# Rectified units made from two ScalarE reads of the PSUM bank and one VectorE instruction, in the first three blocks of a fused attention and two-layer kernel

## The chip, the cores and the metric

The kernel runs on one core of one Trainium2 chip. The metric is device time in microseconds (us), from one launch. A run is one execution; the number for a kernel is the median of its runs. One more execution, taken by the hardware profiler, gives the trace: a record of each instruction with its engine, start and duration. The engines are TensorE (PE, with its weight loads PEld), VectorE (DVE), ScalarE (ACT), GpSimd (POOL) and SyncE (SP), and each works through its own instructions strictly in order. "SPq" and "ACTq" rows are the issues of DMAs on those engines' queues.

## What is computed

Causal attention with a bias made from running sums, then two feed-forward layers on the 2304 tokens (4 sequences of 576, 512 columns). The change is in the second layer, where `h` is rectified with a slope `alpha` of its own for each of the 2048 hidden columns:

```python
# first layer: 1536 hidden columns
a = x @ w_a
b = x @ w_b
x = a * b @ w_out
# second layer: 2048 hidden columns
h = x @ w_in
g = np.maximum(h, 0.0) + alpha * np.minimum(h, 0.0)
return (g @ w_out).astype(np.float32)
```

## The kernel before

The tokens go through the two layers in four blocks: three of 512 tokens (function `ffn`) and one of 768 (`ffn_seven`). The attention of block b+1 is cut into steps that are dealt out between the matrix products of block b; only the first block's attention stands alone, in the first 49 us. Every number that enters a large product is split into a high part (rounded to the matmul's type) and the rest, so `x`, `g` and the weights are pairs (`xh`/`xl`, `gh`/`gl`, `wh`/`wl`) and one product is three matmuls: L1237 to L1239 in the helper `mm3`, or L1888 to L1890 where the second layer leaves its result with tokens on partitions.

In one block the first layer takes 12 turns and the second 16. A turn `f` of the second layer is `into(f % 2)`: 12 matmuls of 512 columns that write `h` for 128 hidden columns into one of two PSUM banks, bank2 for even f and bank3 for odd f (`ab[0]`, `ab[1]`; in the instruction lists below their names end in `_101` and `_102`); then, from the third turn on, the 12 matmuls of the product with `w_out` for turn f-2. PE may write a bank again only when `used[j]`, the chain that reads it, is done. With two banks and two turns before the first `w_out` product, the third turn needs bank2 back while the second is computed; later turns have 12 more matmuls in between.

The chain that reads the bank is `rectify` (L1833 to L1846): ScalarE writes `m = relu(-h)` from the bank (`act`, L286), the helper `scale` (L321) multiplies `m` by `-alpha` on VectorE or GpSimd, and VectorE's scalar_tensor_tensor (L302) reads the bank a second time and makes `g = max(h, 0) + m`. After it `split_g` makes `gh` on ScalarE (L294) and `gl` on VectorE or GpSimd (L311). `m`, `g`, the first layer's `a_sb` and the results `o` that go out share four buffers (`ft`, tag "t", slots `of_t`).

The order of instructions on every engine is set when the program is built, by a planner (class `Order`): every operation has a planned cost on each engine that may do it, is given to the engine that would end it first, and takes its place in the lists by planned start. Operations marked `dve2` hold, with GpSimd's, a common resource "port" in the plan; those marked `dve` don't. A change of one planned cost can so reorder all that is planned after it, and also pick another engine for operations that the change doesn't name. Weights arrive in the first block as 64-bit numbers (`raw<-in_w_dram`), are decoded by ACT (`top`, L1018) and DVE (`raw` or `w`, L302), split into `wh`/`wl`, and stored back to DRAM (`w_d<-raw`, `w_d<-w`, on ACT's queue) for the later blocks. All loads and the stores of results are on SP's queue, in order.

The fourth block has a `rectified_parts` of its own (L1443), which already makes both halves on ScalarE, with `less_alpha = -alpha`, computed at L1316 when that block opens.

Of the kernel before, what the change touches and what calls it, by code (L numbers as in the profile page):

```python
# [15 lines left out]
AF = mybir.ActivationFunctionType  # L16
ALU = mybir.AluOpType
# [204 lines left out]
def attention_two_moe_kernel(  # L222
# [10 lines left out]
    nc = tc.nc  # L233
# [41 lines left out]
    run = Order()  # L275
# [5 lines left out]
    def size(ap):  # L281
        return prod(ap.shape[1:])

    def act(o, i, func=AF.Copy, **k):
        yield {"act": run.act + 0.833 * size(o) + 93 * len(set(k) - {"scale"})}, SEEN
        nc.scalar.activation(o, i, func, **k)  # L286
# [13 lines left out]
    def dve(n, rate, f, *args, port=False, **k):  # L300
        yield {"dve2" if port else "dve": run.dve + rate * n}, SEEN
        f(*args, **k)  # L302

    def either(pool, dve2):
        return {"dve2": dve2} if run.no_pool else Either(pool=pool, dve2=dve2)
# [12 lines left out]
    def scale(o, i, s0, s1):  # L318
        n = size(o)
        eng = yield either(115 + 1.09 * n, dve2=run.dve + 0.52 * n), SEEN  # L320
        (nc.gpsimd if eng == "pool" else nc.vector).tensor_scalar(  # L321
            o, i, s0, s1, op0=ALU.mult, op1=ALU.mult
        )
# [27 lines left out]
    less_alpha = small.tile([P, NF2], F32, name="less_alpha", bufs=1)  # L351
    alpha_sb = small.tile([P, NF2], F32, name="alpha_sb", bufs=1)
# [32 lines left out]
    for i in range(0, P, BH):  # L385
# [4 lines left out]
        op1=ALU.mult,  # L390
# [278 lines left out]
    def both(b, hp, rs):  # L669
        for j in range(2):  # L670
            biases(b, 2 * hp + j, rs)
# [213 lines left out]
    def first_attention():  # L885
        nonlocal ahead
        s_sb = work.tile([BH, S], F32, name="s_sb", tag="z4")
        for i in range(WARM):
            nc.tensor.matmul(acc[0][:, 0:P], ident, ident, start=True, stop=True)
        nc.scalar.activation(alpha_sb[:, 0:1], ident[:, 0:1], AF.Exp)  # L890
        nc.sync.dma_start(s_sb, s)
        for i in range(2):
            load_kq(0, i, 0)
        run.now = 2000.0
        run.pump()
        ahead = EARLY_TILES
        prefetch()
        run.now = 3000.0
        run.pump()
        for i in range(2, HP):  # L900
            load_kq(0, i, 0)
        load_v(0)
        run.pump()
        running_sums(s_sb)
        run.now = 5000.0
        lead, steps = plan[0]

        def scores(i):
            both(0, i, (0, 1))
            both(0, i, (2,))  # L910
            both(0, i, (3,))
            s01(0, i)
            s23(0, i, 2)
            s23(0, i, 3)

        def turns(i):
            for c in range(3):
                for j in range(2):
                    turn(0, 2 * i + j, c)

        def of_steps(n):
            for f, args in steps[:n]:
                f(*args)
            del steps[:n]

        scores(0)
        nc.sync.dma_start(alpha_sb, alpha)
        nc.sync.dma_start(cum_d, cum[0:BH, 0:S])
        scores(1)
        ahead = AHEAD  # L930
        prefetch()
        f, args = lead.pop(0)
        f(*args)
        scores(2)
        turns(0)
        scores(3)
        for x, j in ((xh, "h"), (xl, "l")):
            x.append(xp.tile([P, KD, 512], F32R, name=f"x{j}1", tag=f"x{j}1"))
        for f, args in lead:
            f(*args)  # L940
        turns(1)
        av(0, 0)
        turns(2)
        av(0, 1)
        turns(3)
        av(0, 2)
        of_steps(STEPS)
        av(0, 3)
        of_steps(STEPS)

    def attention(a):

# [354 lines left out]
    def open_seven():  # L1307

        inner.close()
        big = ctx.enter_context(tc.tile_pool(name="big", bufs=1))  # L1310

        def big_tile(shape, dtype, tag, bufs=1):
            return big.tile(shape, dtype, name=tag, tag=tag, bufs=bufs)

        pools["big"] = big_tile
        nc.vector.tensor_scalar(less_alpha, alpha_sb, -1.0, None, op0=ALU.mult)  # L1316
        t_hl[:] = [
            [big_tile([P, 2, H2], F32R, f"t{j}{i}") for j in "hl"] for i in range(4)
        ]
        for slots, n in ((of_m, 4), (of_a22, 2), (of_mt, 2), (of_st, 2), (of_d, 5)):  # L1320
            for _ in range(n):
                run.give(slots)
# [465 lines left out]
    def ffn(blk):  # L1788
        T = sizes[blk]
# [43 lines left out]
        def rectify(f, hp):  # L1833
            yield of_t
            m = ft.tile([P, T], F32, name="m", tag="t")
            yield from act(m, hp, AF.Relu, scale=-1.0)
            yield from scale(m, m, alpha_sb[:, f:f + 1], -1.0)
            yield of_t
            g = ft.tile([P, T], F32, name="g", tag="t")
            yield from dve(  # L1840
                T, 1.04, nc.vector.scalar_tensor_tensor, g, hp, 0.0, m, op0=ALU.max, op1=ALU.add
            )
            run.give(of_t, run.t)
            split_g(f, g)
# [61 lines left out]
    for blk in range(NB):  # L1906
# [5 lines left out]
        T = sizes[blk]  # L1912
# [78 lines left out]
```

## Time and profile before

| | us |
|---|---|
| median of 3 runs | 982.25 |
| lowest and highest run | 981.21, 983.04 |
| the profiled execution's own time | 982.93 |
| its span, first to last instruction | 981.1 |

| engine | busy us | share of the span |
|---|---|---|
| PE | 965.5 | 98% |
| DVE | 748.9 | 76% |
| ACT | 551.6 | 56% |
| POOL | 224.8 | 23% |

Busy shares are means over the whole program. The blocks follow each other at about 49, 265, 500 and 706 us, and the second layers of the first three begin at about 162, 385 and 611 us. A matmul's record is longer than the time to the next one's start, because they are pipelined; what PE lost is read from the starts.

### The profile page before, as it was taken

What the parts mean: (1) busy time and instruction counts of PE and PEld (TensorE: products, weight loads), DVE (VectorE), ACT (ScalarE), POOL (GpSimd) and SP (SyncE); (2) the same over time, 40 slices, a digit from 0 to 9 for tenths busy, and PEclk for the clock granted to TensorE, in tenths of its full rate; (3) what the DMA queues carried; (4) which work ended last, traced back from release to release, by engine and by line L of the source; (5) the groups of instructions that cost most, each with busy time, mean ns of one, the idle gap of its engine ahead of it and who ended that gap; (6) DMA issues with size and microseconds to landing.
All of it is one profiled execution on the core that took longest, in us unless ns stands there. A gap on an engine that the chain in (4) does not pass through costs nothing.

```text
span 981.1 us, 15781 instructions
## 1 busy us (share of the span) xinstructions
PE 965.5 (98%) x5267; PEld 811.4 (83%) x5267; DVE 748.9 (76%) x1714; ACT 551.6 (56%) x1155; POOL 224.8 (23%) x286
## 2 busy tenths in 40 slices
PE   7999999999999999999999999999999999999997
PEld 6677877788878887888888888888899999999896
DVE  8897869877779788777577667975597888787782
ACT  7866766666656556644455455654452333576453
POOL 3141112311245254722044243640000000000000
PEclk9999999999999999999999999999999999999999
DMA  7489997989899898485696867445313223021202
GB/s 264 135 294 328 371 353 243 320 278 330 268 324 299 261 319 252 160 277 168 180 280 202 268 211 221 163 156 164 116 34 96 65 65 104 27 65 65 65 1 64
DMA packets 128065, 192.69 MB, mean 196 GB/s; under 512 B 34288, under 2 KB 65520, under 8 KB 127984
## 3 DMA queue, kind: packets, MB, share of 16 engines
q1 hardware_dynamic: 118192, 173.86, 55.5%
q10 hardware_dynamic: 9792, 17.83, 4.9%
q8 instruction: 41, 0.67, 0.3%
q14 instruction: 40, 0.33, 0.1%
HBM read 148.06 MB, written 43.59 MB: 195 GB/s over the span
## 4 chain that ended last, share of the span: by engine, by line
PE 89%; DVE 4%; DMA 4%; ACT 2%; issue 1%; ACTq 0%; SPq 0%; POOL 0%; POOLq 0%; DVEq 0%
PE bank L1237 20%; PE bank L1238 20%; PE bank L1239 20%; PE bank L1888 4%; PE bank L1889 4%; PE bank L1890 4%; PE bank L842 3%; PE bank L1741 2%; PE bank L1740 2%; PE bank L1742 2%; PE bank L579 2%; DMA cb<-cum_d 1%; DMA raw<-in_w_dram 1%; PE bank L777 1%; DVE z L302 1%; PE bank L869 1%
## 5 line engine op out<-in xcount | busy, mean ns | idle before, releaser
L1237 PE MATMUL bank<-xh,wh 128*128 128x512 f32 (+1 forms) x620 | 238.7, 385 | 4.9 <-ACT a_sb L294 1.7
L1238 PE MATMUL bank<-xl,wh 128*128 128x512 f32 (+1 forms) x620 | 234.3, 378 | 0.0
L1239 PE MATMUL bank<-xh,wl 128*128 128x512 f32 (+1 forms) x620 | 234.3, 378 | 0.0
L294 ACT ACTIVATE wh<-raw 128x512 fp32r<-128x512 f32 (+1 forms) x199 | 116.6, 594 | 145.6 <-PE bank L1238 59.1
L1237 PEld LDWEIGHTS bank<-xh,wh 128*128 128x128 f32 x620 | 116.4, 188 | 29.8 <-issue 3.0
L311 DVE TENSOR_TENSOR wl<-raw,wh 128x512 fp32r<-128x512 f32 (+1 forms) x148 | 97.3, 670 | 51.5 <-ACT wh L294 50.8
L1239 PEld LDWEIGHTS bank<-xh,wl 128*128 128x128 f32 x620 | 116.4, 188 | 19.5
L1238 PEld LDWEIGHTS bank<-xl,wh 128*128 128x128 f32 x620 | 116.5, 188 | 18.4
L286 ACT ACTIVATE z<-z,mn 128x128 f32<-128x128 f32 (+4 forms) x144 | 82.7, 576 | 20.1 <-DVE mn L302 19.4
L311 POOL TENSOR_TENSOR wl<-raw,wh 128x512 fp32r<-128x512 f32 x56 | 75.5, 1349 | 69.7 <-ACT wh L294 64.4
L1237 PE MATMUL bank<-gh,wh 128*128 128x512 f32 (+1 forms) x240 | 90.3, 376 | 0.0
L1238 PE MATMUL bank<-gl,wh 128*128 128x512 f32 (+1 forms) x240 | 88.8, 370 | 0.1
L1239 PE MATMUL bank<-gh,wl 128*128 128x512 f32 (+1 forms) x240 | 88.5, 369 | 0.0
L1888 PE MATMUL bank<-wh,gh 128*128 128x512 f32 x192 | 77.0, 401 | 0.0
L1889 PE MATMUL bank<-wl,gh 128*128 128x512 f32 x192 | 74.9, 390 | 0.0
L1890 PE MATMUL bank<-wh,gl 128*128 128x512 f32 x192 | 74.9, 390 | 0.0
L1018 ACT ACTIVATE top<-raw 128x512 f16<-128x512 bf16 x82 | 63.2, 785 | 20.1 <-DMA raw<-in_w_dram 18.5
L311 DVE TENSOR_TENSOR gl<-g,gh 128x512 fp32r<-128x512 f32 x70 | 55.6, 795 | 20.2 <-ACT gh L294 19.7
L294 ACT ACTIVATE gh<-g 128x512 fp32r<-128x512 f32 x83 | 51.9, 625 | 30.2 <-DVE g L302 28.3
L311 POOL TENSOR_TENSOR wl<-w,wh 128x512 fp32r<-128x512 f32 x26 | 35.1, 1354 | 113.9 <-ACT wh L294 84.6
L302 DVE STREAM_TRANSPOSE zt<-z 128x384 f32<-128x384 f32 (+2 forms) x88 | 55.5, 647 | 3.1 <-DMA zd<-zt 2.0
L652 POOL TENSOR_SCALAR_AFFINE_SELECT z<-z 128x128 f32<-128x128 f32 (+2 forms) x80 | 34.4, 438 | 97.2 <-DVE z L642 47.0
(156 smaller groups left out, 1930.0 us busy)
## 6 DMA issues: line engine op xcount, KB each, us to landing
raw<-w_d SPq DMA_DIRECT2D x95, 512.0 KB, 4.6
raw<-in_w_dram SPq DMA_DIRECT2D x82, 512.0 KB, 6.4
w_d<-w ACTq DMA_DIRECT2D x54, 256.0 KB, 6.2
kq<-in_kq_a_dram SPq DMA_DIRECT2D x24, 512.0 KB, 5.9
zd<-zt SPq DMA_DIRECT2D x48, 192.0 KB, 4.1
pt<-zd SPq DMA_DIRECT2D x48, 192.0 KB, 4.7
zd<-zt SPq DMA_DIRECT2D x24, 256.0 KB, 2.7
pt<-zd SPq DMA_DIRECT2D x24, 256.0 KB, 4.9
```

Source lines behind the costliest of these rows:

```text
L286: nc.scalar.activation(o, i, func, **k)
L294: nc.scalar.activation(o, i, AF.Copy, scale=by)
L302: f(*args, **k)
L311: (nc.gpsimd if eng == "pool" else nc.vector).tensor_tensor(o, i0, i1, op=ALU.subtract)
L652: nc.gpsimd.affine_select(d, d, pattern=pattern, base=0, channel_multiplier=1, compare_op=ALU.is_ge, fill=MASKED,)
L1018: nc.scalar.activation(top.bitcast(F16).rearrange("p (n t) -> p n t", t=2)[:, :, 1], r.bitcast(BF16)[:, 4:4 + 4 * WN].rearrange("p (n t) - ...
L1237: nc.tensor.matmul(o, wh, ih, start=first, stop=False)
L1238: nc.tensor.matmul(o, wh, il, start=False, stop=False)
L1239: nc.tensor.matmul(o, wl, ih, start=False, stop=last)
L1888: nc.tensor.matmul(acc[t], gh[:, c], wh, start=first, stop=False)
L1889: nc.tensor.matmul(acc[t], gh[:, c], wl, start=False, stop=False)
L1890: nc.tensor.matmul(acc[t], gl[:, c], wh, start=False, stop=last)
```

## The change

`rectify` now has ScalarE read the bank twice: `m = relu(-h)` and `g = relu(h)`. The separate scaling is gone. A new chain, `rectified`, is started when both are written: VectorE's scalar_tensor_tensor takes `m`, multiplies it by `less_alpha` and adds `g`, with both tensors in SBUF. The bank's reader chain `used[f % 2]` ends with ScalarE's second read. The new instruction is planned as `dve`, without the port. `less_alpha` is computed at the end of `first_attention` instead of when the fourth block opens.

```diff
@@ first_attention
         av(0, 3)
         of_steps(STEPS)
+        nc.vector.tensor_scalar(less_alpha, alpha_sb, -1.0, None, op0=ALU.mult)
@@ open_seven
-        nc.vector.tensor_scalar(less_alpha, alpha_sb, -1.0, None, op0=ALU.mult)
@@ ffn: rectify
             yield from act(m, hp, AF.Relu, scale=-1.0)
-            yield from scale(m, m, alpha_sb[:, f:f + 1], -1.0)
             yield of_t
             g = ft.tile([P, T], F32, name="g", tag="t")
+            yield from act(g, hp, AF.Relu)
+            run.spawn(rectified(f, m, g), run.t, run.ffn)
+
+        def rectified(f, m, g):
             yield from dve(
-                T, 1.04, nc.vector.scalar_tensor_tensor, g, hp, 0.0, m, op0=ALU.max, op1=ALU.add
+                T, 1.04, nc.vector.scalar_tensor_tensor, g, m, less_alpha[:, f:f + 1], g,
+                op0=ALU.mult, op1=ALU.add,
             )
             run.give(of_t, run.t)
             split_g(f, g)
```

The lists of the two built programs are the same up to the first rectified tile (but for `less_alpha`), differ on every engine from there to the end of the third block, and end alike. Over the program ACT has 42 instructions more (48 times `g`, less six that other engines now do), DVE 20 fewer and POOL 22 fewer; PE has the same matmuls and as many changes between kinds of them.

ACT where the first block's second layer begins, in the kernel before (numbers behind names tell instances apart; `top` is the decoding of a weight tile, `w32` a decoded one):

```order
L286 ACTIVATE m_2001<-bank2_101 128x512
L294 ACTIVATE wh_1999<-w32_1884 128x512
L1018 ACTIVATE top0_150<-raw_1898 128x512
L1018 ACTIVATE top1_151<-raw_1926 128x512
L294 ACTIVATE wh_2038<-w32_1908 128x512
L286 ACTIVATE m_2041<-bank3_102 128x512
```

and now:

```order
L286 ACTIVATE m_2002<-bank2_101 128x512
L294 ACTIVATE wh_2000<-w32_1885 128x512
L286 ACTIVATE g_2012<-bank2_101 128x512
L1019 ACTIVATE top0_150<-raw_1899 128x512
L1019 ACTIVATE top1_151<-raw_1927 128x512
L294 ACTIVATE gh_2033<-g_2012 128x512
L286 ACTIVATE m_2044<-bank3_102 128x512
```

The second read of bank2 stands one `wh` behind the first; the read of bank3 stands behind `gh`, which waits for VectorE's new instruction.

ACT where the second block's second layer begins, before:

```order
L286 ACTIVATE m_4514<-bank2_101 128x512
L286 ACTIVATE z_4352,sm_4498<-z_4352,mn_4497 128x512
L286 ACTIVATE z_4353,sm_4500<-z_4353,mn_4499 128x512
L294 ACTIVATE wh_4512<-raw_4302 128x512
L286 ACTIVATE m_4546<-bank3_102 128x512
```

and now (`kh`, `qs`: parts of the next block's keys and queries; `z`: rows of its scores):

```order
L286 ACTIVATE m_4506<-bank2_101 128x512
L294 ACTIVATE qs_4489<-kq_4144 128x512
L286 ACTIVATE g_4512<-bank2_101 128x512
L286 ACTIVATE z_4352,sm_4495<-z_4352,mn_4494 128x512
L286 ACTIVATE m_4542<-bank3_102 128x512
L294 ACTIVATE gh_4537<-g_4512 128x512
L286 ACTIVATE g_4548<-bank3_102 128x512
```

One `qs` stands between the two reads of bank2.

DVE at the end of the first block, before (`raw_2795` is the decoding of a weight tile, which a store on ACT's queue then waits for; `gl_2992` belongs to the block's last rectified tile, `g_2973`):

```order
L302 SCALAR_TENSOR_TENSOR g_2973<-bank3_102,m_2951 128x512
L311 TENSOR_TENSOR ovl_112<-bank0_99,ovh_111 128x64
L311 TENSOR_TENSOR wl_2950<-raw_2768,wh_2949 128x512
L311 TENSOR_TENSOR gl_2992<-g_2973,gh_2991 128x512
L302 SCALAR_TENSOR_TENSOR raw_2795<-raw_2795,top1_151 128x512
```

and now:

```order
L302 SCALAR_TENSOR_TENSOR g_2964<-m_2953,less_alpha_97,g_2964 128x512
L311 TENSOR_TENSOR wl_2952<-raw_2768,wh_2951 128x512
L302 SCALAR_TENSOR_TENSOR raw_2793<-raw_2793,top1_151 128x512
L311 TENSOR_TENSOR gl_2983<-g_2964,gh_2982 128x512
L311 TENSOR_TENSOR ovl_112<-bank0_99,ovh_111 128x64
```

The decoding stands ahead of `gl` and `ovl` instead of behind them.

## Rows read from the trace of the kernel before

**Rows 1.** PE's waits: engine, line, waited for: us in total, times, longest us

```profile
PE bank L1237 <- ACT a_sb L294: 1.7, 1, 1.7
PE bank L1237 <- DVE sm L302: 1.6, 1, 1.6
PE bank L1237 <- DVE g L302: 1.4, 1, 1.4
```

**Rows 2.** Timeline, first block, second layer's begin: start us, us, engine, line, op, tiles

```profile
165.46 2.69 POOL L311 TENSOR_TENSOR wl<-w,wh 128x512 fp32r<-128x512 f32 x2 [0.17 <-PE bank L1239]
165.43 0.60 ACT L286 ACTIVATE m<-bank 128x512 f32<-128x512 f32 x1
165.92 0.62 ACT L294 ACTIVATE wh<-w 128x512 fp32r<-128x512 f32 x1
166.92 1.52 DVE L321 TENSOR_SCALAR m<-m,alpha_sb 128x512 f32<-128x512 f32 x1
168.85 0.65 DVE L302 SCALAR_TENSOR_TENSOR g<-bank,m 128x512 f32<-128x512 f32 x1
167.50 0.39 PE L1238 MATMUL bank<-xl,wh 128*128 128x512 f32 x1
167.72 0.39 PE L1239 MATMUL bank<-xh,wl 128*128 128x512 f32 x1
169.55 0.50 PE L1237 MATMUL bank<-xh,wh 128*128 128x512 f32 x1 [1.44 <-DVE g L302]
```

**Rows 3.** Timeline, second block, second layer's begin

```profile
387.40 0.60 ACT L286 ACTIVATE m<-bank 128x512 f32<-128x512 f32 x1 [0.39 <-PE bank L1239]
390.98 0.68 DVE L302 SCALAR_TENSOR_TENSOR g<-bank,m 128x512 f32<-128x512 f32 x1
389.71 0.39 PE L1239 MATMUL bank<-xh,wl 128*128 128x512 f32 x1
391.72 0.50 PE L1237 MATMUL bank<-xh,wh 128*128 128x512 f32 x1 [1.61 <-DVE sm L302]
```

**Rows 4.** Timeline, first block to second: the chain to the third wait

```profile
246.25 0.78 ACT L646 ACTIVATE z<-cb,cumq 128x576 f32<-128x576 f32 x1 [2.61 <-DMA cb<-cum_d]
249.95 0.48 DVE L321 TENSOR_SCALAR m<-m,alpha_sb 128x512 f32<-128x512 f32 x1
259.08 0.68 DVE L311 TENSOR_TENSOR gl<-g,gh 128x512 fp32r<-128x512 f32 x1
259.68 0.68 DVE L302 SCALAR_TENSOR_TENSOR raw<-raw,top 128x512 int32<-128x512 int32 x1
260.39 0.33 ACTq L1174 DMA_DIRECT2D w_d<-raw  x1
265.56 0.97 SPq L327 DMA_DIRECT2D out_dram<-o  x2
270.84 0.60 ACT L294 ACTIVATE a_sb<-bank 128x512 f32<-128x512 f32 x1 [5.52 <-DMA out_dram<-o]
269.37 0.40 PE L1239 MATMUL bank<-xh,wl 128*128 128x512 f32 x1
271.49 0.50 PE L1237 MATMUL bank<-xh,wh 128*128 128x512 f32 x1 [1.73 <-ACT a_sb L294]
```

**Rows 5.** Groups by form: xcount, busy us, mean ns, idle before

```profile
L286 ACT ACTIVATE m<-bank 128x512 f32<-128x512 f32 x48 | 28.0, 584 | 9.3 <-PE bank L1239 8.9 <-DVE sm L302 0.3
L302 DVE SCALAR_TENSOR_TENSOR d<-mt,less_alpha,d 128x768 f32<-128x768 f32 x12 | 12.0, 1011 | 1.6 <-ACT d L286 1.6
```

**Rows 6.** Tiles m and g: xcount: duration ns min/median/max, first, last start

```profile
L302 DVE SCALAR_TENSOR_TENSOR g<-bank,m x48: 646/691/692, 168.8 to 700.5; 128x512 f32<-128x512 f32 x48
L321 DVE TENSOR_SCALAR m<-m,alpha_sb x39: 443/482/1519, 166.9 to 700.0; 128x512 f32<-128x512 f32 x39
L311 DVE TENSOR_TENSOR gl<-g,gh x70: 644/692/1783, 64.7 to 702.9; 128x512 fp32r<-128x512 f32 x70
```

**Rows 7.** First block, second layer: us, PE, PEld, DVE, ACT, POOL busy, PEclk, DMA

```profile
160.00:260.00 100.00, 98.56 (x508) 79.05 (x506) 79.82 (x159) 67.28 (x125) 25.65 (x30) 1.00 0.91 308
```

## The prediction

> **What bounds the kernel.** I read PE's waits first. After the opening attention (the first 49 us) that view has three entries, one each of 1.4, 1.6 and 1.7 us [rows 1]; everywhere else PE starts one 512-column matmul after the other, 0.22 to 0.23 us apart, as at 167.50 and 167.72 [rows 2]. So PE's own work sets the time, and since the change leaves the matmuls as they are, it can win at most what PE loses in these places, and can lose whatever new waits it makes. The timeline around each shows what they are.
>
> The first is where the first block's second layer begins [rows 2]. The third turn wants bank2, and its first matmul could have started at 167.72 + 0.23 = 167.95; it starts at 169.55, when VectorE's `g` (168.85 + 0.65 = 169.50) has read the bank. Lost: 1.60. The bank was long in the hands of a chain over three engines: `m` at 165.43, a scaling of 1.52 us on VectorE beside a GpSimd stretch of 2.69, a transpose, then `g`.
>
> The second is the same place of the second block [rows 3]: 389.71 + 0.23 = 389.94, and PE starts at 391.72, just after `g` ended (390.98 + 0.68 = 391.66; the view names a `sm` that ended later, but the bank's reader is `g`). Lost: 1.78.
>
> The third is the step from the first block to the second [rows 4], and is no rectified tile: bank2 has to be copied to `a_sb`, which needs one of the four shared buffers, and these hold results until their store has landed. PE could go at 269.37 + 0.23 = 269.60 and goes at 271.49. Lost: 1.89. Followed back, `a_sb` (270.84) waits for the store issued at 265.56, which stands on SP's queue behind a weight load that needs the buffer of a weight tile, whose own store was issued at 260.39, after its decoding on VectorE (259.68). That VectorE stretch in turn starts behind a load that ScalarE waited for until 246.25.
>
> In all 1.60 + 1.78 + 1.89 = 5.27 us are to be had.
>
> **The change, part by part.** ScalarE's second read: 48 instructions of the form of `m`, so 48 x 0.584 = 28.0 us of ScalarE [rows 5], 16 x 0.584 = 9.3 in each block's second layer. In the first block's stretch ScalarE is busy 67.28 of 100 us [rows 7]; with it 76.6. That is off the path as long as ScalarE has its third of idle time; what it costs without that cover is a rival below.
>
> Taken away: 48 scalings, 39 on VectorE at a median of 0.482 [rows 6] and 9 on GpSimd. In the stretch where VectorE is busy 79.82 of 100 us [rows 7] that frees some 5 us; no gain by itself, since PE waits for VectorE nowhere but at the gates.
>
> The bank's release. In the first block ScalarE reads at 165.43, the `wh` behind it starts 0.49 later at 165.92, the second read another 0.5 later, at about 166.4, and ends by 167.0 [rows 2, 5], nearly 1 us ahead of the 167.95 at which PE wants the bank. VectorE and GpSimd are no longer in that chain. All 1.60 go. In the second block one `qs` stands between the reads: 387.40 + 0.5 + 0.5 = 388.4, end at 389.0, again nearly 1 us ahead of 389.94 [rows 3]. All 1.78 go. What is late next is the other bank: ScalarE's read of bank3 now stands behind `gh`, which waits for VectorE's new instruction. PE comes back to bank3 only after 24 more matmuls (12 into bank2, 12 with `w_out`), 24 x 0.225 = 5.4 us later, and the two reads and a `gh` are 3 x 0.6 = 1.8; I cost it at nothing.
>
> The new VectorE instruction, `g = m * less_alpha + g`, has both tensors in SBUF, and the trace has no 512-wide one. From below, the same operation of the fourth block, 768 wide at 1011 ns with GpSimd idle [rows 5], gives 1011 x 512 / 768 = 674; from above stand 1783, the longest of the `gl`, which also read two SBUF tensors [rows 6]. I take 0.69, the median of the `gl`, since most of them are undisturbed. The old form read the bank and one SBUF tensor and never took more than 692 in 48 times, whatever GpSimd did [rows 6]. So the new form is open to GpSimd where the old one wasn't; against that the scaling, which was open too (443 to 1519), is gone.
>
> The Trainium skill, "SBUF — State Buffer", section "Who interferes with whom", states just this: a VectorE instruction with two SBUF inputs contends with a GpSimd instruction that reads SBUF, and one with at most one SBUF input, outside the two-port modes, doesn't. It speaks against the change. The rows agree: by that rule the sum moves as in the second rival below; without it the new instruction would always cost 0.69.
>
> The step between the blocks decides what is left of the first 1.60. PE arrives there earlier, but `a_sb` follows its own chain, so the first block's net gain is what that chain moves, from 0 up to 1.60 + 1.89 = 3.49. VectorE's part of the chain loses a scaling (0.48 at 249.95), and the decoding now stands ahead of the last `gl`, worth 259.68 - 259.08 = 0.60 [rows 4]: 1.1 earlier by that. If the start of the stretch, a load on SP's queue, also follows PE by 1.60, it is 2.7; if new places in the lists eat it, 0. I take 1.5, a little above the part that is read from rows, since the loads' buffers are released by engines that partly follow PE.
>
> Everything else in the lists between 165 and 706 us is reordered too: many operations change engine or place. PE has had no wait in all that stretch but the three, and VectorE and GpSimd have less to do, so I expect little; bounds are 0 and about one more wait of the size of the three, 1.9. I take 0.5, a quarter of one such wait. `less_alpha` earlier costs one tiny instruction; nothing waits for it.
>
> Sum: -1.5 - 1.78 + 0.5 = -2.8 us, so 982.93 - 2.8 = 980.1 for an execution like the profiled one, whose span is 981.1 with 1.8 around it. That execution was 0.7 above the median of 982.25, so the forecast for the median is 982.25 - 2.8 = 979.5.
>
> **Rivals.** (a) The first block's gain is handed back: `a_sb` doesn't move, PE just waits 3.49 there instead of 1.89. For it: the chain starts from a load, which doesn't know of PE. Against: two of its VectorE items go. Then -1.78 + 0.5 = -1.3, 981.0.
>
> (b) GpSimd holds up the new instruction in that chain. Two of them stand in VectorE's stretch before the decoding; each may take up to 1.78 - 0.69 = 1.09 more [rows 6], together 2.2 against the 1.1 won, so `a_sb` comes 1.1 later, and PE with it: 1.1 - 1.78 + 0.5 = -0.2, 982.1. For it: GpSimd is busy a quarter of the stretch [rows 7], and the planner doesn't keep its work away from the new instruction. Against: the scaling had the same exposure. This is the mechanism of the page named above.
>
> (c) The third wait goes too: the chain moves by 2.7 or more, the first block gains 3.49 at best, -3.49 - 1.78 = -5.3, 977.0.
>
> (d) Slower: ScalarE becomes the bound of the first block's second layer. Its queue is in order, and two thirds busy is already with waits of its own in it; if its idle time is all waits that stay, the 9.3 us add up there instead of hiding, in both banks' releases, the weights' high parts and `gh`: 9.3 - 1.60 - 1.78 = +5.9, 988.2. It decides when ScalarE's work in a turn passes PE's: with 76.6 of 100 us it doesn't on the mean, so it takes a crowd in which a third of its time is lost. Against it too: no PE wait but `a_sb`'s is for ScalarE.
>
> (e) The change doesn't do what it says: the bank's second read stands late in ScalarE's queue, and waits of the old size turn up at other gates; 982.3.
>
> **How the numbers follow.** The forecast (978 to 980.5) has 0.50, (a) 0.18, (b) 0.10, (c) 0.10, (d) 0.07, (e) 0.05. About 0.2%, 2.0 us, is what a measurement of this kernel tells from no change, so faster means under 980.3. The forecast gives 0.46 of its 0.50 to faster and (c) all; with a little of (a), faster is 0.60; (a), (b), (e) and the rest of the forecast make within 0.2% 0.32; slower is (d) with a little of (e), 0.08. The range goes from (c)'s 977.0 to 982.6, just above (b) and (e); only (d) and the outermost of (c) lie beyond.
>
> **What would show it.** In the new profile PE's waits should have no entry for `g` at the begin of the second layers, and bank2 should be released by ScalarE's `g<-bank` near 167.0 and 389 (less what came before). The wait for `a_sb` should still be there, 1 to 3 us, with its store issued about 1.5 earlier than 265.56. The new VectorE instruction should have a median of 0.67 to 0.70 and a tail to 1.8. ScalarE should be busy some 77 of 100 us in the first block's second layer without PE waiting for it. Wrong would be: a PE wait for `wh`, `gh` or a bank read by ScalarE in those layers (d), a longer wait for `a_sb` that takes the 1.60 back (a, b), or several new waits of 1 us in the reordered stretch (e).

## The result, and the profile after

The changed kernel takes 989.2 us (median of 4 runs, 988.45 to 991.68), against 982.11 for the kernel before in the same job: a ratio of 1.0074, 95% interval 1.0062 to 1.0086. It is slower by 7.1 us where the prediction said faster by 2.8, and outside its range. The profiled execution took 988.54, with a span of 986.8 (before: 982.93 and 981.1). L1237 to L1239 of before are now L1238 to L1240, and L1018 and L1174 are L1019 and L1175.

PE's waits, as in [rows 1] (engine, line, waited for: us in total, times, longest us):

```profile
PE bank L579 <- DVE mn L302: 2.4, 2, 1.9
PE bank L579 <- DVE ovl L311: 2.3, 1, 2.3
PE bank L777 <- DVE ovl L311: 1.0, 1, 1.0
PE bank L1238 <- ACT a_sb L294: 0.4, 1, 0.4
```

The entries for `g` and `sm` of [rows 1] are gone and the one for `a_sb` has shrunk from 1.7 to 0.4. Three entries that did not exist have come, four waits of 2.34, 0.96, 1.92 and 0.48 us: L579 and L777 are the score steps of the next blocks' attention, which stand between the products of the second block's **first** layer. That layer has no rectified tile, so not one of its instructions is changed.

What was forecast did happen. The timeline at the place of [rows 2] (start us, us, engine, line, op, tiles): ScalarE's second read ends at 166.82 + 0.59 = 167.41, and the third turn starts at 168.32 on PE's even beat.

```profile
165.80 0.60 ACT L286 ACTIVATE m<-bank 128x512 f32<-128x512 f32 x1
166.82 0.59 ACT L286 ACTIVATE g<-bank 128x512 f32<-128x512 f32 x1
168.10 0.39 PE L1240 MATMUL bank<-xh,wl 128*128 128x512 f32 x1
168.32 0.39 PE L1238 MATMUL bank<-xh,wh 128*128 128x512 f32 x1
```

And what was not: the timeline around 318 us.

```profile
317.56 0.33 PE L579 MATMUL bank<-kl,qs 128*128 128x384 f32 x1
320.23 0.44 PE L579 MATMUL bank<-kh,qs 128*128 128x384 f32 x1 [2.34 <-DVE ovl L311]
321.73 0.63 PE L1238 MATMUL bank<-xh,wh 128*128 128x512 f32 x1
322.16 0.63 PE L1239 MATMUL bank<-xl,wh 128*128 128x512 f32 x1
324.57 0.40 PE L1239 MATMUL bank<-xl,wh 128*128 128x512 f32 x1
324.80 0.40 PE L1240 MATMUL bank<-xh,wl 128*128 128x512 f32 x1
319.95 0.23 DVE L311 TENSOR_TENSOR ovl<-bank,ovh 128x64 fp32r<-128x64 f32 x1 [5.01 <-ACT ovh L294]
318.42 0.77 ACT L646 ACTIVATE z<-cb,cumq 128x576 f32<-128x576 f32 x1 [5.72 <-DMA pt<-zd]
319.73 0.19 ACT L294 ACTIVATE ovh<-bank 128x64 fp32r<-128x64 f32 x1
```

Read upwards: ScalarE stands 5.7 us before a bias `z<-cb` whose operand, a row of running sums, is still being loaded. (The bracket names the load of a `pt`; the instruction itself reads `cb`.) Behind it in ScalarE's queue stands a copy of 0.19 us, `ovh`, and for that VectorE's `ovl`, and for that the bank that PE wants for its next score step. The place costs more than the wait: after it the matmuls start 0.43 us apart instead of 0.23 (321.73, 322.16) until 324.57. The line numbers of the traces below differ a little from run to run, since the edits add lines.

### The profile page after: what moved, and what is told of

Read it like the earlier page. It is cut to its first block, busy times and chain, and to the rows that moved or that the text cites. A ratio compares the mean times of both kernels' runs of the same rounds, so it can differ in the third digit from the quotient of the medians.

```text
span 986.8 us, 15762 instructions
## 1 busy us (share of the span) xinstructions
PE 969.8 (98%) x5267; PEld 813.6 (82%) x5267; DVE 743.7 (75%) x1694; ACT 572.8 (58%) x1197; POOL 204.7 (21%) x264
## 4 chain that ended last, share of the span: by engine, by line
PE 91%; DVE 3%; DMA 3%; ACT 1%; issue 1%; SPq 0%; POOL 0%; ACTq 0%; POOLq 0%; DVEq 0%
PE bank L1238 20%; PE bank L1239 20%; PE bank L1240 20%; PE bank L1892 5%; PE bank L1893 4%; PE bank L1894 4%; PE bank L842 3%; PE bank L1741 2%; PE bank L1740 2%; PE bank L1742 2%; PE bank L579 2%; PE bank L777 1%; PE bank L598 1%; DVE z L302 1%; DMA pt<-zd 1%; PE bank L869 1%
## 5 line engine op out<-in xcount | busy, mean ns | idle before, releaser
L1238 PE MATMUL bank<-xh,wh 128*128 128x512 f32 (+1 forms) x620 | 239.6, 387 | 0.5 <-ACT a_sb L294 0.4
L1240 PE MATMUL bank<-xh,wl 128*128 128x512 f32 (+1 forms) x620 | 235.2, 379 | 0.0
L1239 PE MATMUL bank<-xl,wh 128*128 128x512 f32 (+1 forms) x620 | 235.1, 379 | 0.0
L1238 PEld LDWEIGHTS bank<-xh,wh 128*128 128x128 f32 x620 | 116.8, 188 | 25.0 <-issue 3.2
L1240 PEld LDWEIGHTS bank<-xh,wl 128*128 128x128 f32 x620 | 116.9, 189 | 19.7
L1239 PEld LDWEIGHTS bank<-xl,wh 128*128 128x128 f32 x620 | 116.8, 188 | 18.7
L1238 PE MATMUL bank<-gh,wh 128*128 128x512 f32 (+1 forms) x240 | 90.2, 376 | 0.0
L1239 PE MATMUL bank<-gl,wh 128*128 128x512 f32 (+1 forms) x240 | 89.3, 372 | 0.1
L1240 PE MATMUL bank<-gh,wl 128*128 128x512 f32 (+1 forms) x240 | 88.8, 370 | 0.0
L311 POOL TENSOR_TENSOR wl<-raw,wh 128x512 fp32r<-128x512 f32 x51 | 70.0, 1376 | 70.8 <-ACT wh L294 41.4
L1892 PE MATMUL bank<-wh,gh 128*128 128x512 f32 x192 | 76.6, 399 | 0.0
L1019 ACT ACTIVATE top<-raw 128x512 f16<-128x512 bf16 x82 | 62.9, 785 | 14.0 <-DMA raw<-in_w_dram 11.3
L652 POOL TENSOR_SCALAR_AFFINE_SELECT z<-z 64x64 f32<-64x64 f32 (+2 forms) x80 | 34.3, 435 | 116.3 <-DVE z L642 60.2
L302 DVE SCALAR_TENSOR_TENSOR w<-raw,top 128x512 int32<-128x512 int32 x68 | 48.5, 725 | 11.7 <-ACT top L1019 9.0
```

The lines of the kernel that those rows point to most:

```text
L311: (nc.gpsimd if eng == "pool" else nc.vector).tensor_tensor(o, i0, i1, op=ALU.subtract)
L652: nc.gpsimd.affine_select(d, d, pattern=pattern, base=0, channel_multiplier=1, compare_op=ALU.is_ge, fill=MASKED,)
L1019: nc.scalar.activation(top.bitcast(F16).rearrange("p (n t) -> p n t", t=2)[:, :, 1], r.bitcast(BF16)[:, 4:4 + 4 * WN].rearrange("p (n t) - ...
L1238: nc.tensor.matmul(o, wh, ih, start=first, stop=False)
L1239: nc.tensor.matmul(o, wh, il, start=False, stop=False)
L1240: nc.tensor.matmul(o, wl, ih, start=False, stop=last)
```

## Experiments

Theory after this comparison: the new instructions do what was forecast; the planner, run again with other costs, has put the attention's work of the second block in an order that makes PE wait. Rival: the new instructions themselves cost it, by ScalarE's load (the prediction's d) or by a slower instruction on VectorE beside GpSimd (its b).

**Instructions and order crossed.** Edit of the changed kernel's `rectify`, so that the planner deals with the old operations and plans the old order while the new instructions are emitted (`e1_old_order`):

```diff
             yield of_t
             g = ft.tile([P, T], F32, name="g", tag="t")
-            yield from act(g, hp, AF.Relu)
-            run.spawn(rectified(f, m, g), run.t, run.ffn)
+            nc.scalar.activation(g, hp, AF.Relu)
+            yield from dve(... g, m, less_alpha[:, f:f + 1], g ...)
+            ...                                   # give and split_g, as before
```

with a planned, empty `yield either(...)` in the old scaling's place ahead of it.

> The changed instructions in the order of the kernel before: the planner is told the old costs, so the rows of PE and SP are word for word those of before, and on the other engines only the 48 second reads come in on ScalarE, the 48 scalings go and the 48 additions take their new form. Theory (the order is to blame): the waits at the begin of the second layers go, no wait of a score step between 310 and 365 us appears, and the time is that of the prediction, 982.1 - 1.8 - 0 to 1.6 = 978.7 to 980.3. Rival (ScalarE's 28 us more, or the new form on VectorE, cost the time): the loss stays, 987 to 990.

The mirror image (`e4_new_order`): at the planned place of the second read, the old scaling and the old addition; the planned place of the new addition stays, empty.

```diff
-            yield from act(g, hp, AF.Relu)
+            yield {"act": run.act + 0.833 * T}, SEEN
+            nc.vector.tensor_scalar(m, m, alpha_sb[:, f:f + 1], -1.0, ...)
+            nc.vector.scalar_tensor_tensor(g, hp, 0.0, m, ...)
+            ...                                   # in rectified: the cost alone
```

> The old instructions in the order of the changed kernel: at the place of each second read of ScalarE, VectorE gets the scaling and the old addition that reads the bank; PE, SP and GpSimd rows are those of the changed kernel. Theory (order): the waits of score steps at 317, 353 and 358 us stay, and those at the begin of the second layers come back on top, 989.2 + 0 to 3.4 = 989 to 993. Rival (the new instructions): with them gone the time is that of before, 981 to 983.

The change in the first block alone, and in the other two alone: `if not (blk == 0):` or `if not (blk > 0):` ahead of the old lines of `rectify`.

> The change in the first block alone. Its order is that of the changed kernel up to the end of the second block's first layer, so theory (order) expects the same waits of score steps at 317, 353 and 358 us, although two thirds of the new instructions are not there: 989.2 + 1.8 for the wait at the begin of the second block's second layer, which is back, = 989 to 992. Rival (new instructions): a third of the loss, 982.1 + 7.1 / 3 = 984.5.

> The change in the second and the third block alone. The order up to the end of the second block's first layer is that of before, so theory (order) expects no wait of a score step there: 982.1 - 1.8 for the second block's gate = 980.3, with 1.5 to either side for what the new order does behind it. Rival (new instructions): two thirds of the loss, 982.1 + 7.1 x 2 / 3 = 986.8.

Medians in us (before: 982.56 in this job; the changed kernel's 989.2 is from its own, where before took 982.11):

| | old order | new order |
|---|---|---|
| old instructions | 982.56 | 991.03 |
| new instructions | 979.01 | 989.2 |

The new instructions in the old order are **faster** than the kernel before, 0.9957 (0.9941 to 0.9973); the old instructions in the new order are as slow as the changed kernel, 1.0078 (1.0062 to 1.0094). So the instructions are worth -3.5 us in the old order and the order +8.5 with the old instructions. In the new order the instructions make no difference that can be told: 1.0074 against 1.0078 of before. The halves agree: first block alone 990.99, with waits for the same three steps, 2.2, 3.6 and 2.4 us; the other two blocks alone 980.97. The rival is out. One point of the expectation for `e4_new_order` missed: the waits at the begin of the second layers did not come back. In the first block the old chain there makes `g` at 166.23 and is done at 166.92, and PE writes the bank at 167.01. The time lies in the range said because the score steps wait longer, 3.3, 2.4 and 1.7 us. So the old instructions too release the banks in time when they stand early enough, and the new ones are one way to it. PE's waits with the new instructions in the old order, after 49 us:

```profile
PE bank L1238 <- ACT a_sb L294: 0.9, 1, 0.9
PE bank L1238 <- ACT g L1840: 0.2, 1, 0.2
```

**What in the order costs it.** First at the places themselves. In `e5_ovh` the one `ovh` of 319.73 is made by VectorE; in `e6_both` also a bias for which VectorE stood 6.1 us until 348.41 is made by GpSimd. Both leave the program's order as it is. The edits, shortened:

```diff
+        if (b, hp) == (0, 2): nc.vector.tensor_copy(hi, src)          # e5, e6: ovh
+        if (b, h, r) == (2, 1, 4): nc.gpsimd.tensor_scalar(o, cb ...) # e6: bias
```

> The changed kernel with one instruction on another engine: the 128x64 copy ovh that ScalarE starts at 319.73 us, behind a bias that waits 5.7 us for its load, is done by VectorE at the same place of the program. Every other row of every engine stays. Theory: the score step at 317.56 no longer waits and the eight matmuls behind it at half rate run at full rate, 989.2 - 2.5 - 1.6 = 985.1 if PE keeps the gain; if the next waits (353, 358 us) are set by a load that does not know of PE, they grow by up to the same amount and the time stays at 987 to 989. Rival (the wait is not ScalarE's queue): the wait at 317.56 stays as long as it is.

> As the run with ovh on VectorE, and the bias of 576 columns that holds VectorE from 342.3 to 348.4 us (it waits for its load) is done by GpSimd at the same place of the program; two instructions in all on another engine, and every other row as in the changed kernel. Theory: the waits at 353.27 (1.1), 357.81 (2.1) and 360.25 (0.6) go or shrink, and so do the matmuls at half rate behind them (1.4), 985.1 - 5.2 = 980 at best; 982 to 984 if GpSimd, now the one that waits for the load, delivers a weight's low part late. Rival (these waits have another cause): 985 to 989.

988.7, 1.0067 (1.0055 to 1.0079), and 986.87, 1.0044 (1.0032 to 1.0056). PE's waits from 300 to 375 us in `e5_ovh`:

```profile
PE bank L777 <- DVE ovl L311: 3.2, 1, 3.2
PE bank L579 <- DVE mn L302: 2.4, 2, 2.0
PE bank L777 <- DVE mn L302: 2.1, 1, 2.1
```

The wait at 317 is gone, and PE, earlier by it, waits 2.1 us at the next step and 3.2 instead of 1.0 at the one after. ScalarE's bias still waits, 6.0 us until 320.7, and delays the decoding behind it, and VectorE behind that. The waits are not made where PE shows them; the loads are late, and whoever is early waits for them elsewhere. `e6_both` was to reach 980 to 984 and missed that in the same way: ScalarE stands 7.4 us before its bias, until 319.35, VectorE behind it, and a wait of 3.5 for `mn` stands at 320.6.

**Where the loads become late.** The stretches 270 to 310 us of before and after (us, PE, PEld, DVE, ACT, POOL busy, PEclk, DMA share, GB/s):

```profile
270.00:310.00 40.00, 38.39 (x188) 31.38 (x189) 32.89 (x86) 25.14 (x55) 18.18 (x22) 1.00 0.99 310
```

```profile
270.00:310.00 40.00, 39.91 (x195) 32.18 (x194) 33.89 (x80) 23.02 (x49) 21.30 (x25) 1.00 0.79 257
```

Before, the DMA engines are busy all the time here; after, a fifth of the time is lost, ahead of the waits. The changed kernel's timeline of VectorE and of SP's queue shows where SP stands still:

```profile
291.44 0.52 DVE L642 TENSOR_SCALAR z<-cb,cumq 128x576 f32<-128x576 f32 x1 [3.64 <-DMA cb<-cum_d]
300.73 2.94 DVE L321 TENSOR_SCALAR z<-z,sm 128x512 f32<-128x512 f32 x2
303.66 1.29 DVE L302 STREAM_TRANSPOSE zt<-z 128x512 f32<-128x512 f32 x2
284.66 0.60 SPq L327 DMA_DIRECT2D cb<-cum_d  x1
297.32 1.32 SPq L327 DMA_DIRECT2D vt<-in_v_dram  x2
304.39 0.34 SPq L327 DMA_DIRECT2D zd<-zt  x1
306.63 0.47 SPq L327 DMA_DIRECT2D cb<-cum_d  x1
310.56 0.89 SPq L327 DMA_DIRECT2D cb<-cum_d  x1
```

VectorE stands 3.6 us until 291.44 for the `cb` issued at 284.66. Behind it in VectorE's queue come, among others, the scaling of two heads' probabilities (`z<-z,sm`) and their transposes at 303.66. SP has a store of the first transpose (`zd<-zt`) next in its queue at 297.32 + 1.32 = 298.6 and issues nothing until 304.39. Behind that store are the two halves of the next `cb` (306.63, 310.56), for which ScalarE then stands until 318.42. An engine waits for a load in order, a store waits for the engine, and the queue with the next loads waits for the store.

The late `cb` is only a part of it. In the kernel before, VectorE gets to the same bias no earlier, at 291.65, but to the transposes after 8.2 us in place of 12.2, and SP's store goes out at 300.69 without a wait:

```profile
291.65 0.52 DVE L642 TENSOR_SCALAR z<-cb,cumq 128x576 f32<-128x576 f32 x1 [0.77 <-DMA cb<-cum_d]
299.17 1.36 POOL L321 TENSOR_SCALAR z<-z,sm 128x512 f32<-128x512 f32 x2 [1.60 <-DVE sm L302]
299.90 1.38 DVE L302 STREAM_TRANSPOSE zt<-z 128x512 f32<-128x512 f32 x2
```

The two `z<-z,sm` are GpSimd's there, 1.36 us for both; the new order gives them to VectorE, where they take 2.94. In `e7_margin`, a kernel further down, the `cb` is as late (VectorE stands 3.71 us until 291.32), but one of the two is GpSimd's, the first transpose starts at 299.63, and SP stands 1.7 us at this store instead of 5.7. No run moves this work alone, and `e7_margin` differs elsewhere too, so what it is worth to PE stays open.

Three kernels test SP's part of that chain by moving single DMAs from SP's queue to ScalarE's at the same place of the program: `e8_zd` the two stores, `e10_cb` the one load, `e11_cb_zd` all three. The edits, shortened:

```diff
+        if (b, h, rs[0]) in ((2, 0, 3), (2, 1, 3)):      # e8, e11
+            nc.scalar.dma_start(zd..., zt)
+                if (b, h, u, j) == (0, 3, 1, 1):          # e10, e11
+                    nc.scalar.dma_start(dst, src)         # half a row of cb
```

> The changed kernel with two stores (zd, of the first two heads' transposed probabilities) issued by ScalarE in place of SP, at the same place of the program; every other row of every engine stays. In the changed kernel SP issues nothing from 298.6 to 304.4 us, since the first of them waits for VectorE, and the DMA engines move 0.38 and 0.70 of their share from 300 to 310. Theory: the loads behind the stores now go out from 299, the bias and the ovh behind it no longer wait at 317, and the waits at 353 and 358 shrink: 980 to 984. Rival (the waits come from the bank readers' places in the lists, not from late loads): the waits at 317 to 360 stay, 987 to 990.

> The changed kernel with one load on another queue: the second half of the row of sums (cb, 64x576) for which VectorE waits 3.6 us until 291.4 is issued by ScalarE at the same place of the program, near 281, in place of SP at 284.7; every other row of every engine stays. Theory (one late load starts it: VectorE 3.6 us late, so the transpose for which SP stands still until 304.4 is late, so all loads behind it, so the waits at 317, 353 and 358): VectorE waits under 1 us, SP stands still 2 to 3 us less, the wait at 317 goes and the two others shrink, 980 to 985. Rival (each wait has its own cause): only VectorE's wait goes and the time stays at 987 to 990.

> The same load and the two zd stores of the earlier run on ScalarE's queue, three DMAs in all on another queue, every other row as in the changed kernel. Theory: the two edits add up as far as there is something left, 979 to 983. Rival (each wait has its own cause): as with the two stores alone, 985 to 987.

The stores alone: 985.87, 1.0043 (1.0026 to 1.0059), less than was expected. The load alone: 984.88, 1.0027 (1.0012 to 1.0042). All three: 979.78, 0.9978 (0.9967 to 0.9989); the whole loss, and faster than before. VectorE and SP's queue in `e10_cb`:

```profile
288.84 0.51 DVE L646 TENSOR_SCALAR z<-cb,cumq 128x576 f32<-128x576 f32 x1
301.16 1.29 DVE L302 STREAM_TRANSPOSE zt<-z 128x512 f32<-128x512 f32 x2
297.30 1.26 SPq L327 DMA_DIRECT2D vt<-in_v_dram  x2
301.89 0.34 SPq L327 DMA_DIRECT2D zd<-zt  x1
```

VectorE no longer waits at the bias, the transposes come 2.5 us earlier, SP stands still for 3.3 us in place of 5.7, and the wait at 317 is gone; 2.0 and 0.8 are left of the others. The `cb` is in time here, so what SP still stands is for VectorE's other work ahead of the transposes. SP's queue in `e11_cb_zd` goes on at once, with the stores out of it (it stands next from 302.1 to 305.5, before a weight load), and PE has one wait place left in the stretch:

```profile
297.00 3.07 SPq L327 DMA_DIRECT2D vt<-in_v_dram  x4
300.18 0.52 SPq L327 DMA_DIRECT2D kq<-in_kq_b_dram  x1
301.67 0.47 SPq L327 DMA_DIRECT2D cb<-cum_d  x1
```

```profile
PE bank L583 <- DVE mn L302: 2.3, 2, 1.8
```

(That execution took 983.07, the longest of its 12, so the median has less.)

Moving three DMAs saved 989.2 - 979.8 = 9.4 us, while their issues in the changed kernel take 0.60, 0.34 and 0.54 us (at 284.66, 304.39 and 307.20). What was saved is not issue time: a DMA that waits for an engine held back every later one on its issuer's queue, 5.7 us at the store above. The Trainium skill, "DMA: Bandwidth & Descriptors", section "Issuing engines are not separate DMA queues", says that starting DMAs from several engines saves only the time that issuing takes. Here page and measurement differ; the section does not speak of a DMA that waits.

The other way round, `e9_more_dma` puts an idle copy of 1.57 MB on SP's queue of `e1_old_order`.

```diff
+        if (b, h, rs[0]) == (2, 0, 3):
+            nc.sync.dma_start(idle_d, w_d[0:6])
```

> The changed instructions in the old order, 979.0, with one more DMA on SP's queue near 298 us that copies 1.57 MB within DRAM (some 5 us of all DMA engines at the 300 GB/s of that stretch) and that nothing reads. Theory (late loads make the waits, in whatever order): waits of score steps or weights of 1 to 4 us appear between 300 and 375 us, 982 to 987. Rival (the old order's lists have the margin): 979 to 980.

984.09, 5.1 more than without it. That supports the theory only in part: a wait of 1.3 for a score step has come at 338, but another one, 1.4 for `gh` until 259.5 us, lies ahead of the copy (299.87) and has another cause.

**How chancy the order is.** Four kernels change one setting of the planner and no operation of the program, though the planner may then give an operation to another engine; `e7_margin` asks for a margin.

```diff
-AS_TRACED = ... (13.3, 170.0, 155.0, -4000.0)
+AS_TRACED = ... (13.3, 172.0, 155.0, -4000.0)   # p4 (changed kernel), p1 (before)
+AS_TRACED = ... (13.3, 170.0, 157.0, -4000.0)   # p5 (changed kernel)
-LATE, LATE_0 = 1000.0, 1300.0
+LATE, LATE_0 = 1010.0, 1310.0                   # p6 (changed kernel)
-        spare = SURE["bank"] if f in (s4, av_b) else -100.0
+        spare = SURE["bank"] if f in (s4, av_b) or not scarce and f in (s01, s23) else -100.0   # e7
```

> The changed kernel, and in the planner ScalarE's fixed cost from the second block on is 172 ns in place of 170, a number that changes no instruction, only the order from some 215 us on. Theory (which order comes out is close to chance): the three waits do not come back as they were; the time is anywhere from 977 to 992, and differs from 989.2 by over 2. Rival (the loss is the work's, not the order's): 988 to 990.

> The changed kernel, with the planner's fixed cost of VectorE 157 ns in place of 155 from the second block on; no instruction changes, 76 of PE's rows stand elsewhere. Theory: between 977 and 992 and over 2 from 989.2; it is slow if the DMA share from 300 to 310 us is under 0.7 as in the changed kernel, and 981 or less if it is over 0.8. Rival: 988 to 990.

> The changed kernel, with the planner's threshold for GpSimd's lateness 1010 ns in place of 1000; no instruction changes, and PE's rows are the same up to 351 us of the changed kernel's trace and again from 362 us on, with 24 rows between them elsewhere. The two settings that gave 978 to 979 change the order from 266 us on. Theory (what is done to the loads between 266 and 350 us decides): the wait at 317 stays and the time stays high, 985 to 990. Rival (any change of the numbers moves it back): 978 to 982.

> The kernel before, with the planner's fixed cost of ScalarE 172 ns in place of 170 from the second block on; no instruction changes, 16 of PE's rows stand elsewhere. Theory (order near chance, but only a small part of it moves here): 981 to 985, with a difference of 0.3 or more from 982. Rival: within 0.3 of 982.

> The changed kernel, with the planner asked to let a score step start only when its bank has been free for 2 us by its own clock (before: not at all), from the second block on; the order changes from 217 us on. Theory: the planner's clock is up to 2.5 us too early for the banks, and with that margin the waits of score steps between 310 and 365 us fall below 0.5 each, giving 980 to 983. Rival (the loads are late by more than that, or the new order makes new waits): 984 to 990.

| kernel | median us | ratio (95%) | DMA share 270 to 310 | PE's waits 300 to 375, us |
|---|---|---|---|---|
| before, in five jobs | 981.97 to 982.56 | 1 | 0.99 | 0 |
| p1, before with 172 | 982.62 | 1.0004 (0.9995 to 1.0013) | 0.95 | 0 |
| p5, changed with 157 | **978.29** | 0.9964 (0.9952 to 0.9976) | 0.90 | 0 |
| p4, changed with 172 | 978.84 | 0.9969 (0.9957 to 0.9981) | 0.90 | 0 |
| new instructions, old order | 979.01 | 0.9957 (0.9941 to 0.9973) | 0.98 | 0 |
| changed, three DMAs moved | 979.78 | 0.9978 (0.9967 to 0.9989) | 0.88 | 2.3 |
| second and third block only | 980.97 | 0.9982 (0.9971 to 0.9993) | 0.92 | 0.6 |
| e7, margin of 2 us | 981.84 | 0.9996 (0.9987 to 1.0006) | 0.90 | 3.4 |
| new instructions, old order, added copy | 984.09 | 1.0022 (1.0012 to 1.0031) | 0.97 | 1.3 |
| changed, cb moved | 984.88 | 1.0027 (1.0012 to 1.0042) | 0.87 | 2.8 |
| changed, two zd moved | 985.87 | 1.0043 (1.0026 to 1.0059) | 0.87 | 4.5 |
| changed, ovh and bias moved | 986.87 | 1.0044 (1.0032 to 1.0056) | 0.78 | 4.3 |
| p6, changed with 1010 | 987.84 | 1.0052 (1.0037 to 1.0067) | 0.79 | 6.6 |
| changed, ovh moved | 988.70 | 1.0067 (1.0055 to 1.0079) | 0.81 | 7.7 |
| **changed** | 989.2 | 1.0074 (1.0062 to 1.0086) | 0.79 | 5.7 |
| first block only | 990.99 | 1.0076 (1.0053 to 1.0098) | 0.84 | 8.2 |
| old instructions, new order | 991.03 | 1.0078 (1.0062 to 1.0094) | 0.82 | 7.4 |

Two nanoseconds in a planned cost take the changed kernel from 989.2 to 978.8 or 978.3. These two orders part from the changed kernel's at about 270 us, and PE's waits never come. The chain is there, only shorter: SP stands 2.0 and 2.5 us at the same store and ScalarE 3.5 and 3.0 before the same bias, and it ends before PE wants the bank. The order of `p6` differs in PE's rows only from 351 to 362 us, behind the first of the waits, and stays slow, as expected. Leaving the added copy aside, every kernel that is slow by over 2 us has a share of 0.87 or less in 270 to 310, and every other one 0.88 or more. It is a trend, no threshold: `p5` was to be fast with a share over 0.8 in 300 to 310, and was fast with 0.79 (0.63 and 0.95). `p1`, with 16 of PE's rows elsewhere, can't be told from before. In `e7_margin` the time fell as expected, but for another reason than expected: waits of 2.4 and 1.0 are still there, and so is VectorE's wait for the late `cb`.

## Why the prediction was wrong, point by point

**The first gate.** Held. Its 1.60 are gone; ScalarE's second read ended at 167.41 where "by 167.0" was said, and ScalarE's first read came 0.37 later than in the trace of before (165.80 for 165.43).

**The second gate.** Held. PE has no wait there after the change; all 1.78 are gone.

**The step between the blocks.** Under-sized for the profiled execution. Net 1.5 was taken for the first block, of 0 to 3.49. There `a_sb` came at 268.17 for 270.84 in [rows 4], and PE lost 0.60 there where it had lost 1.89: 1.60 + 1.29 = 2.9 for the block. Its store went out at 262.44 for 265.56, so the chain moved by 2.7, rival (c)'s amount. The profile:

```profile
268.17 0.60 ACT L294 ACTIVATE a_sb<-bank 128x512 f32<-128x512 f32 x1 [4.54 <-DMA out_dram<-o]
268.82 0.50 PE L1238 MATMUL bank<-xh,wh 128*128 128x512 f32 x1 [0.44 <-ACT a_sb L294]
```

This one varies: in the seven executions whose order is the changed kernel's up to here (its own, `e5_ovh`, `e6_both`, `e8_zd`, `e10_cb`, `e11_cb_zd`, `p6`) PE waits 0.36 to 1.80 us for `a_sb`, which makes the block's gain about 1.5 to 3.0. So 1.5 is its lower end.

**ScalarE's load.** Held: ScalarE is busy 76.92 of 100 us in the stretch of [rows 7] (160 to 260), where 76.6 was worked out, and PE waits for no rectified tile. So (d) named nearly the right time for a wrong reason; the same load in the old order gives 979.

**The new instruction.** Its price was too low, but that did not decide. Taken was 0.69; it takes 752 ns at the median and never under 703, with a tail past the bound of 1783:

```profile
L302 DVE SCALAR_TENSOR_TENSOR g<-m,less_alpha,g x48: 703/752/1978, 167.4 to 706.0; 128x512 f32<-128x512 f32 x48
```

The old form never took more than 692 [rows 6]. In this trace 32 of the 48 run beside no GpSimd instruction and take 703 to 753, so the higher median is not GpSimd's doing; the ten that take longer, 836 to 1978, all run beside one. By the Trainium skill, "SBUF — State Buffer", section "Who interferes with whom", such a tail is what an instruction with two SBUF inputs has to fear from a GpSimd instruction that reads SBUF; the trace agrees. But (b) is not the loss: the same instruction, 705/752/1647, stands in the kernel of 979.01.

**The reordering: the step that failed.** "Everything else in the lists between 165 and 706 us is reordered too ... bounds are 0 and about one more wait of the size of the three, 1.9. I take 0.5." This term of the sum, +0.5, was +9.5 by the trace; by the crossed kernels it was +8.5 with the old instructions and 989.2 - 979.0 = 10.2 with the new. In the changed kernel's trace it is made of the waits beyond the even beat at 317.56, 353.27, 357.81 and 360.25, which are 2.5 + 1.1 + 2.1 + 0.6 = 6.3, and, after the first and after the last two, a stretch of half rate, each 3.6 us for 9 matmul starts that take 2.04 at 0.227, so 2 x 1.6. That is 9.5, against gains of 2.9 + 1.78 = 4.7; the net of 4.8 is most of the 5.7 between the spans, and 0.37 more lay ahead of the first gate.

The bound was read from a wrong place. "PE has had no wait in all that stretch but the three" says how the old order went, not what another would do. What should have set it: DMA share 0.99 in 270 to 310 with loads, stores and engines waiting for one another in order, so that a lost microsecond is not made up soon; and that the planner picks all such work afresh from the first rectified tile on. Without that term the sum is 982.25 - 1.5 - 1.78 = 978.97, and the new instructions in the old order measured 979.01. That the two are so close is partly luck: the measured gain is 982.56 - 979.01 = 3.55 for the 3.28 of the sum, and one of its two parts varies by 1.5 from execution to execution. Rival (e) had half of the mechanism, "waits of the old size turn up at other gates", but as equal exchange, 982.3 with 0.05, and with the bank's second read standing late, which it did not. It should have had a side far above, since one stretch of SP's queue can hold up several score steps: the one late `cb` alone, moved, brought back 989.2 - 984.88 = 4.3 us, and the three DMAs 9.4.

**Settled and open.** Shown, by the crossed kernels: the order costs the time, not the instructions. Shown, by the three moved DMAs: it does so through what stands still on SP's queue. `p6` agrees that the damage is done before 351 us, but changes too little behind it to prove that. Not shown: which decision of the planner starts it. The two `z<-z,sm` on VectorE and the late `cb` are the candidates, and no run undoes the first. Why `e9_more_dma` has a wait ahead of its copy stays open too.

The best version is the changed kernel with 157 in place of 155: 978.29, 0.9964 of before. `p4`, the old order and the three moved DMAs are within 1.5 us of it, so what is gained is probably the change's own 3 to 4 us.

## What to carry to other kernels

Where a planner sets the order, a local change is two changes, and the second may be the larger: try the new instructions in the old order first, which here tells the instructions' -3.5 us from the order's +8.5, and then look for an order. In a stretch whose DMA share is near 1, look at the in-order queue of the loads first: here a store in it that waited for an engine held every later load from 298.6 to 304.4 us, and PE's waits showed up later, from 317.6 to 361 us, and somewhere else. Removing a wait where PE shows it may only move it, as in `e5_ovh`, as long as what is late behind it stays late.

## What the runs showed of the hardware that was not expected

A short wait of PE can cost more than itself. Stretches behind the first and the third wait of the changed kernel, columns as above:

```profile
320.00:326.00 6.00, 5.77 (x19) 4.64 (x20) 5.21 (x15) 3.55 (x9) 0.92 (x3) 0.72 1.06 381
362.00:366.00 4.00, 4.00 (x12) 3.10 (x12) 3.02 (x14) 2.80 (x11) 2.99 (x3) 0.58 0.99 361
```

The granted clock is 0.72 and 0.58 of full speed there, 0.43 us from start to start, which is the lower of the two levels, 1.2 GHz; the rest of the stretch is at 2.4. It fell after waits of 2.34 us and of 1.92 and 0.48, and full speed was back some 3.6 us later, so the wait of 2.3 us cost 3.9. After the wait of 0.96 at 354.64 it did not fall:

```profile
354.64 0.75 PE L777 MATMUL bank<-kq 128*128 128x288 f32 x2 [0.96 <-DVE ovl L311]
355.46 0.39 PE L1239 MATMUL bank<-xl,wh 128*128 128x512 f32 x1
355.68 0.40 PE L1240 MATMUL bank<-xh,wl 128*128 128x512 f32 x1
```

The three waits of before, 1.4 to 1.7 us, had no such stretch behind them either (granted clock 1.00 in 169 to 174, 271 to 276 and 391 to 396), so the rows of before show no such price, and the prediction has no term for it.

The length of a wait does not decide it alone. In `e2_first_block` PE waits 2.18, 3.65 and 1.96 us until 319.81, 355.35 and 360.82, the second longer than any wait of the changed kernel, and the granted clock stays at 1.00 behind each (319 to 326, 355 to 360 and 361 to 367); so it does in `e5_ovh` after 2.15, 3.21 and 1.96. The stretch behind the longest of them:

```profile
355.00:360.00 5.00, 3.52 (x14) 2.48 (x14) 4.92 (x10) 1.55 (x3) 1.32 (x2) 1.00 0.50 170
```

What else decides it stays open. These two kernels are as slow as the changed one without any stretch of half rate, so the waits alone can cost as much.
